# Moving one of three shifted additions from VectorE to GpSimd in an attention kernel

## The chip, the cores and the metric

The kernel runs on one core of one Trainium2 chip. The metric is the device time of one execution in microseconds (us). In the profile PE is TensorE (PEld its weight loads), DVE is VectorE, ACT is ScalarE, POOL is GpSimd, SP the engine that issues the DMAs. PSUM is the memory that PE writes its results to (the tiles psA, psD and psO here), SBUF the memory of all other tiles. The granted clock is the mean share of its full clock that PE was given in a run. A name such as L754 is a line of the kernel's source.

All full kernels were run two to four times, always next to runs of the kernel before on the same chip, and are compared with fast runs only; no run of them was slow (over 1.5% above the fastest of its kernel). A ratio of two kernels is the mean time of one kernel's runs over the mean of the other's of the same rounds, so it isn't quite the ratio of the medians that are quoted.

## The reference

```python
# B, H, S, Dh = 1, 32, 2048, 20; bfloat16
qn = q / (jnp.sqrt((q * q).sum(axis=-1, keepdims=True)) + eps)
kn = k / (jnp.sqrt((k * k).sum(axis=-1, keepdims=True)) + eps)
logits = jnp.einsum('bhqd,bhkd->bhqk', qn, kn) * t[None, :, None, None]
attn = _softmax(logits, axis=-1)
return jnp.einsum('bhqk,bhkd->bhqd', attn, v)
```

The heads are small (20 columns), so most of the work of ScalarE and VectorE is the exponential of 32 x 2048 x 2048 scores.

## The kernel before

Scores are made on PE in blocks of 128x512, 2048 blocks in all. Most go through ScalarE's exponential. The rest are taken by VectorE in tiles of four blocks, and it makes the exponential with integer arithmetic: it reads the scores from PSUM, scales them and writes int16 numbers that are, taken as fp16 bits, a piecewise linear 2^x. To smooth that curve, three copies of the tile are shifted by a quarter, a half and three quarters of an octave. PE sums all four, with the value rows scaled to undo the shift. This is that part (`# ...` marks cuts):

```python
PHASES = (256, 512, 768)
def add_dgroup(jg):
    # ... per tile two reads of PSUM, 1024 columns each:
    t1_prev[nchunk[0]] = add("DVE", f"t1.{j}.{k}", lambda e, tk, o=o, slot=slot: e.tensor_scalar(
        xt[sx][:, o:o + W1], psD[:, slot * W1:slot * W1 + W1], X_MUL, X_ADD, ALU.mult, ALU.add), ...)
    # ... three shifted copies of 2048 columns:
    sh = [dv(f"s{i}.", lambda e, tk, i=i: e.tensor_scalar(
        ss[i][se][:, 0:w], x, float(PHASES[i]), None, ALU.add), 0.533, ...) for i in range(len(PHASES))]
    # ... four groups of value matmuls, one for xt and one for each ss
```

GpSimd does little: it scales the value rows once for each head and phase.

```python
vsc[h] = [add("POOL", f"vs{h}", lambda e, tk, i=i: e.tensor_scalar(
    vph[bv][:, i, 0:nd, :], vaug[bv][:, R - nd:R, :], 2.0 ** (-PHASES[i] / 1024.0), 1.0, ALU.mult, ALU.mult), 0.5, ...)]
```

The kernel orders its instructions with a list scheduler of its own, which is given a duration for every task (the number after the function, in us) and emits a fixed order for each engine.

Of the kernel before, what the change touches and what calls it, by code (L numbers as in the profile page):

```python
# [26 lines left out]

class Task:
    __slots__ = ("eng", "fn", "dur", "deps", "pri", "name", "lat", "dma", "n", "users",
                 "start", "end", "seq", "inc", "cnt", "rows", "work", "modes")  # L30

    def __init__(self, eng, name, fn, dur, deps, pri, lat=0.0, dma=None):
        self.eng, self.name, self.fn, self.dur = eng, name, fn, dur
        self.deps = [d for d in deps if d is not None]
        self.pri, self.lat, self.dma = pri, lat, dma
        self.inc, self.cnt = False, 0
        self.rows, self.work, self.modes = 128, 512.0, None


class Program:  # L40
# [23 lines left out]
    def schedule(self):  # L64


        heavy = set()
        choice = [t for t in self.tasks if t.modes]
        for _ in range(self.PASSES):
            for t in choice:  # L70
                tag, t.rows, t.dur, t.work = t.modes[t in heavy]
                t.name = tag + t.name[2:]
            self.list_schedule()
            pe = [t for t in self.order["PE"] if t.end > self.LIGHT]
            more, i, load = set(), 0, 0.0
            work = [t.work for t in pe]
            for j, t in enumerate(pe):
                while pe[i].end < t.end - self.TICK:
                    load -= work[i]
                    i += 1  # L80
                for free in (True, False):
                    m = j - 1
                    while i and load < self.LOAD and m >= i:
                        u = pe[m]
                        if u.modes and u not in heavy and u not in more and (u.modes[1][2] == u.dur) == free:
                            more.add(u)
                            work[m] += u.modes[1][3] - u.work
                            load += u.modes[1][3] - u.work
                        m -= 1
                load += work[j]  # L90
            if not more:
                break
            heavy |= more
        self.heavy = heavy
        return self.order

    def list_schedule(self):
        for t in self.tasks:
            t.users = []
        for i, t in enumerate(self.tasks):  # L100
            t.seq = i
            deps = []
            for d in t.deps:
                deps += d() if callable(d) else [d]
            t.deps = list(dict.fromkeys(deps))
            t.n = len(t.deps)
            for d in t.deps:
                d.users.append(t)
        free = {}
# [15 lines left out]
        for t in self.tasks:  # L125
# [3 lines left out]
            if t.n == 0:  # L129
                arrive(t, 0.0)  # L130
        order = {e: [] for e in free}
        done = 0
        last_pe = [""]
        while events:
            now = events[0][0]
            touched = set()
            while events and events[0][0] <= now:
                _, kind, _, t = heapq.heappop(events)
                touched.add(t.eng)
                if kind == 0:  # L140
                    heapq.heappush(ready[t.eng], (t.pri, t.seq, t))
                    if t.eng in soon:
                        soon[t.eng].pop(t.seq, None)
            for e in touched:
                if free[e] > now + 1e-9 or not ready[e]:
                    continue
                held = []
                if e in soon:
                    held = [r for r in ready[e] if r[2].name[:2] not in ("t1", "tr") and
                            not (e == "PE" and r[2].name[0] == "q" and r[2].name[2] == "A") and hold(e, now, r[2].dur)]  # L150
                    if len(held) == len(ready[e]):
                        continue
                    if held:
                        ready[e] = [r for r in ready[e] if r not in held]
                        heapq.heapify(ready[e])
                if e == "PE":
                    x = min(ready[e], key=lambda r: (r[0] + (0.0 if r[2].name[:2] == last_pe[0] else self.SWITCH), r[1]))
                    ready[e].remove(x)
                    heapq.heapify(ready[e])
                    t = x[2]  # L160
                else:
                    _, _, t = heapq.heappop(ready[e])
                for r in held:
                    heapq.heappush(ready[e], r)
                t.start = now
                t.end = now + t.dur
                if e == "PE":
                    kind = t.name[:2]
                    if kind != last_pe[0]:
                        t.end += 0.09  # L170
                        self.nsw += 1
                    if now < self.PE_REST:
                        t.end += t.dur
                    last_pe[0] = kind
                free[e] = t.end
                order[e].append(t)
                done += 1
                heapq.heappush(events, (t.end, 1, t.seq, t))
                for u in t.users:
                    lat = t.lat if t.dma else (  # L180
                        self.SEM_LAT[e] if u.eng != e else 0.12 if e == "DVE" else 0.0)
                    if u.eng == "PE" and u.name[:2] == "pv":
                        lat += self.PV_SLACK
                    rt[u.seq] = max(rt[u.seq], t.end + lat)
                    u.n -= 1
                    if u.n == 0:
                        arrive(u, rt[u.seq])
        assert done == len(self.tasks), "dependence cycle"
        self.order = order
        return order  # L190
# [57 lines left out]
def bass_standalone__qk_norm__prompt_kernel(  # L248
# [13 lines left out]
    W1 = 1024  # L262
    LIGHT3 = True
    NP = 40
    NB = 6
    NV = 6
    NN = 4
    NT = 3
    NX = 4
    NE = 3  # L270
    GD = 1
    NWARM2 = 5
    NWARM = 15
# [4 lines left out]
    FIRST = -7.0  # L278
    DLEAD = 0.8
    PE_MM = 0.23  # L280
    MORE = 10
    DVE_TILES = [4 + (h * MORE // 31 > (h - 1) * MORE // 31 if h else 0) for h in range(H)]
    NDMAX = 5

    with ExitStack() as es:
        sbuf = lambda name, shape, dt: es.enter_context(nc.sbuf_tensor(name, shape, dt))
# [27 lines left out]
        prog = Program()  # L314
        add = prog.add

        def dma(eng, name, dst, src, deps, pri, key, lat=2.2, dur=0.62):
            return add(eng, name, lambda e, tk: e.dma_start(dst, src), dur, deps, pri, lat=lat, dma=key)  # L318

        def memset(eng, ap, val, dur, pri):  # L320
# [65 lines left out]
        def add_loads(h):  # L386
            b, bv = h % NB, h % NV
            pri = h - LEAD - 0.5
            war = ([norm[h - NB]] if h >= NB else []) + ([lambda: [trn[h - 2]]] if h >= EARLY else [])
            x = qk_sb[b]  # L390
            lds[h] = [dma("SP", f"ldk{h}", x[:, R:2 * R, :], k[0, h].rearrange("(p r) d -> p r d", p=128),
                          war, pri - 0.01 if h else -50, f"k{b}")]
            if h == 0:
                lds[h].append(dma("ACT", "ldq0", x[:, 0:R, :], q[0, 0].rearrange("(p r) d -> p r d", p=128),
                                  [], -99, "q0a"))
            else:

                for nh in range(4):
                    src = bass.AP(q.tensor, q[0, h].offset + nh * D,
                                  [[16 * D, 32], [4 * D, 4], [512 * D, 4], [1, D]])  # L400
                    dst = x[32 * nh:32 * nh + 32, 0:R, :].rearrange("p (c g) d -> p c g d", g=4)
                    lds[h].append(dma("SP", f"ldq{h}", dst, src, war, pri, f"q{b}", lat=2.5))
            war = (pv_users[h - NV] if h >= NV else z_v[bv]) + ([lambda: [trn[h - 2]]] if h >= 2 else [])
            if h == 1:
                war = war + [lambda: [trn[0]]]
# [2 lines left out]
            nd = NDMAX if h == 0 else DVE_TILES[h]  # L408
            vsc[h] = [add("POOL", f"vs{h}", lambda e, tk, i=i: e.tensor_scalar(  # L409
                vph[bv][:, i, 0:nd, :], vaug[bv][:, R - nd:R, :], 2.0 ** (-PHASES[i] / 1024.0), 1.0, ALU.mult, ALU.mult),  # L410
                0.5, [ld_v[h]] + (pv_users[h - NV] if h >= NV else z_v[bv]), pri + 0.2) for i in range(len(PHASES))]

        def add_prep(hs):
            due = hs[0] - LEAD if hs[0] != 1 else FIRST
# [46 lines left out]
        def add_trn(h):  # L461
# [2 lines left out]
            war = [lambda: qk_users[h - NT] + rot[h - NT]] if h >= NT else []  # L464
            trn[h] = add("SP", f"trn{h}", lambda e, tk: e.dma_start_transpose(
                qkT[bt][:, :].rearrange("p (c n) -> p c n", n=128),
                qkn[b][:, :, :].rearrange("p r d -> p (r d)")), 1.3, [norm[h]] + war, due + 0.1, lat=2.2, dma=f"T{bt}")
            rot[h] = [dma("SP", f"qz{h}", qz[bt][32 * g:32 * g + 32, g, :], qkT[bt][32 * g:32 * g + 32, 0:512],
                          [trn[h], z_qz[bt]] + ([lambda: qk_users[0]] if h == NT else []), due + 0.15, f"Z{bt}") for g in range(NG)]

# [179 lines left out]
        def add_dgroup(jg):  # L650
# [32 lines left out]

            def dv(name, fn, dur, deps):
                return add("DVE", f"{name}{js[0]}", fn, 0.068 + dur * len(js), deps, due)
            sh = [dv(f"s{i}.", lambda e, tk, i=i: e.tensor_scalar(  # L686
                ss[i][se][:, 0:w], x, float(PHASES[i]), None, ALU.add), 0.533, t1s + old(f"s{i}", NE)) for i in range(len(PHASES))]
            dusers["x", jg] = list(sh)
            for nm, tile, dep, ph in [("x", xt[sx], t1s, None)] + [(f"s{i}", ss[i][se], [sh[i]], i) for i in range(len(PHASES))]:
                us = dusers.setdefault((nm, jg), [])  # L690
                for i, j in enumerate(js):
                    h, rg = D_tiles[j]
# [82 lines left out]
```

## Time and profile before

| kernel before | |
|---|---|
| time, median of the first three runs | 711.08 us (710.19 to 712.51) |
| ScalarE busy | 689.1 us, 97% of the profiled span of 712.0 us |
| VectorE busy | 684.5 us, 96% |
| PE / GpSimd busy | 633.1 us / 37.8 us |
| VectorE tiles | 138 of four blocks each |

The engine totals of the page (busy us, share of the span, number of instructions):

```profile
PE 633.1 (89%) x5715; PEld 168.6 (24%) x5780; DVE 684.5 (96%) x1041; ACT 689.1 (97%) x607; POOL 37.8 (5%) x116
```

The groups of instructions by shape (columns: line, engine, operation, out<-in, shapes and types, count, then busy us and mean ns of one, then idle time of the engine before them and what ended it):

```profile
L632 ACT ACTIVATE p_ring<-psA 128x1536 bf16<-128x1536 f32 x299 | 450.9, 1508 | 14.5 <-PE psA L546 13.5
L678 DVE TENSOR_SCALAR xt<-psD 128x1024 int16<-128x1024 f32 x276 | 335.5, 1216 | 7.6 <-PE psD L546 7.4
L632 ACT ACTIVATE p_ring<-psA 128x1024 bf16<-128x1024 f32 x299 | 324.6, 1086 | 2.0 <-PE psA L546 1.7
L686 DVE TENSOR_SCALAR ss<-xt 128x2048 int16<-128x2048 int16 x414 | 270.5, 682 | 0.1
...
L409 POOL TENSOR_SCALAR vph<-vaug 128x128 f16<-128x128 bf16 x63 | 22.5, 357 | 402.6 <-DMA vaug<-in_v_dram 399.3
...
L409 POOL TENSOR_SCALAR vph<-vaug 128x160 f16<-128x160 bf16 x33 | 12.2, 368 | 212.9 <-DMA vaug<-in_v_dram 211.2
```

ScalarE and VectorE are both full. To win time, work has to leave both: if VectorE gets lighter, tiles can move to it from ScalarE. In the last two lines GpSimd scales value rows, 128 elements in 357 ns and 160 in 368 ns.

Who waited for whom (total us, times, longest us):

```profile
ACT p_ring L632 <- PE psA L546: 15.2, 27, 1.7
DVE xt L678 <- PE psD L546: 7.4, 10, 2.0
...
DVE sq L426 <- DMA qk_sb<-in_q_dram: 5.5, 5, 2.2
```

The waits of the two full engines are small. Last, two stretches of the timeline (start us, duration us, engine and instruction). They show where GpSimd and VectorE meet:

```profile
303.87 0.69 DVE L686 TENSOR_SCALAR ss<-xt 128x2048 int16<-128x2048 int16 x1
303.91 1.54 POOL L409 TENSOR_SCALAR vph<-vaug 128x128 f16<-128x128 bf16 x3 [39.32 <-DMA vaug<-in_v_dram]
...
348.90 1.22 DVE L678 TENSOR_SCALAR xt<-psD 128x1024 int16<-128x1024 f32 x1
349.44 1.05 POOL L409 TENSOR_SCALAR vph<-vaug 128x128 f16<-128x128 bf16 x3 [39.55 <-DMA vaug<-in_v_dram]
350.03 0.81 DVE L428 TENSOR_REDUCE rs_sum<-sq 128x32 f32<-128x640 bf16 x1
```

Three scalings of GpSimd took 1.54 us where a shift of VectorE had started just ahead of them, and 1.05 us under a PSUM read and a reduction. This fits what the Trainium skill, "SBUF — State Buffer", section "Who interferes with whom", says of the port of SBUF that both engines share: a VectorE operation in a two-port mode and a GpSimd operation exclude each other, while one with at most one input from SBUF, outside of these modes, leaves the port to GpSimd. That a shift is of the first kind and a PSUM read of the second is at this point only suggested by the two stretches; e1 tests it.

### The profile page before, as it was taken

The page shows a single profiled execution, that of the slowest core. Times are in us where ns is not written, and L with a number is a line of the kernel's source. Part 1 is how long each engine was busy: PE and PEld are TensorE (multiplying, and loading weights), DVE is VectorE, ACT ScalarE, POOL GpSimd, SP SyncE. Part 2 cuts the span into 40 slices and gives each one's busy share as a digit, 9 for nine tenths or more (in the row PEclk, how much of TensorE's full clock was granted, in tenths as well). Part 3 has the DMA queues.
Part 4 walks back from the last instruction along what each step waited for, and adds up shares of the span by engine and source line. Part 5 has one row for each costly group of instructions (what it writes and reads, how often), then busy time and mean ns, then how long its engine had stood idle before and what let it go on. Part 6 is the DMA issues. An engine that isn't in the chain of part 4 may idle for free.

```text
span 712.0 us, 14025 instructions
## 1 busy us (share of the span) xinstructions
PE 633.1 (89%) x5715; PEld 168.6 (24%) x5780; DVE 684.5 (96%) x1041; ACT 689.1 (97%) x607; POOL 37.8 (5%) x116
## 2 busy tenths in 40 slices
PE   7888988898899988888989999898999899999897
PEld 2222222222222222222222222222222222222221
DVE  8999899998999999999999989999999899999996
ACT  8999999999899999999999999999999989999997
POOL 3010000101001010010100101000010000100000
PEclk9999999999999999999999999999999999999999
DMA  5332413334143241322413234241332513322100
GB/s 64 71 49 42 74 17 90 33 71 57 23 81 30 68 55 37 70 22 68 60 31 74 29 75 48 50 67 27 78 36 53 69 25 74 35 68 47 39 17 10
DMA packets 196720, 36.20 MB, mean 51 GB/s; under 512 B 172592, under 2 KB 196656, under 8 KB 196656
## 3 DMA queue, kind: packets, MB, share of 16 engines
q1 hardware_dynamic: 196512, 35.22, 30.1%
q8 instruction: 45, 0.74, 0.4%
q14 instruction: 19, 0.16, 0.1%
q10 hardware_dynamic: 144, 0.08, 0.0%
HBM read 7.87 MB, written 2.62 MB: 15 GB/s over the span
## 4 chain that ended last, share of the span: by engine, by line
DVE 41%; SPq 34%; ACT 11%; DMA 6%; issue 5%; PE 3%; ACTq 0%; DVEq 0%
SPq L318 34%; DVE xt L678 19%; DVE ss L686 12%; ACT p_ring L632 11%; DMA qk_sb<-in_q_dram 4%; DVE qkn L454 3%; DVE rs_sum L428 2%; DMA qkT<-qkn 1%; DVE sq L426 1%; DVE oT L577 1%; PE psA L546 1%; DVE o_stage L587 1%; PE psO L565 1%; PE psD L546 1%; DVE rs_b L438 1%
## 5 line engine op out<-in xcount | busy, mean ns | idle before, releaser
L632 ACT ACTIVATE p_ring<-psA 128x1024 bf16<-128x1024 f32 x599 | 682.3, 1296 | 16.5 <-PE psA L546 15.2
L678 DVE TENSOR_SCALAR xt<-psD 128x1024 int16<-128x1024 f32 x276 | 335.5, 1216 | 7.6 <-PE psD L546 7.4
L546 PE MATMUL psA<-qz,kR 64*128 64x512 bf16 (+2 forms) x1100 | 252.3, 385 | 23.0 <-ACT p_ring L632 17.4
L686 DVE TENSOR_SCALAR ss<-xt 128x2048 int16<-128x2048 int16 x414 | 270.5, 682 | 0.1
L565 PE MATMUL psO<-ss,vph 128*32 128x512 f16 x1656 | 152.7, 386 | 6.5 <-DVE ss L686 6.3
L565 PE MATMUL psO<-p_ring,vaug 128*32 128x512 bf16 x1496 | 133.8, 385 | 1.1 <-ACT p_ring L632 1.1
L546 PE MATMUL psD<-qz,kR 64*128 64x512 bf16 (+1 forms) x384 | 112.6, 386 | 24.0 <-DVE xt L678 16.0
L546 PE MATMUL psA<-qz,qkT 64*128 64x512 bf16 (+2 forms) x366 | 119.8, 384 | 9.7 <-ACT p_ring L632 7.1
L546 PEld LDWEIGHTS psA<-qz,kR 64*128 64x128 bf16 (+2 forms) x1122 | 59.3, 93 | 168.1 <-ACT p_ring L632 147.4
L409 POOL TENSOR_SCALAR vph<-vaug 128x128 f16<-128x128 bf16 (+1 forms) x96 | 34.6, 361 | 615.6 <-DMA vaug<-in_v_dram 610.5
L565 PEld LDWEIGHTS psO<-ss,vph 128*32 128x32 f16 x1656 | 37.7, 94 | 92.2 <-issue 52.2
L546 PE MATMUL psD<-qz,qkT 64*128 64x512 bf16 (+1 forms) x133 | 50.9, 386 | 8.5 <-DVE xt L678 4.7
L565 PE MATMUL psO<-xt,vaug 128*32 128x512 f16 x552 | 53.1, 390 | 0.1
L565 PEld LDWEIGHTS psO<-p_ring,vaug 128*32 128x32 bf16 x1496 | 35.7, 94 | 61.9 <-issue 51.4
L546 PEld LDWEIGHTS psD<-qz,kR 64*128 64x128 bf16 (+1 forms) x414 | 27.9, 95 | 86.2 <-DVE xt L678 78.0
L546 PEld LDWEIGHTS psA<-qz,qkT 64*128 64x128 bf16 (+2 forms) x374 | 29.8, 93 | 62.2 <-ACT p_ring L632 56.0
L577 DVE STREAM_TRANSPOSE oT<-psO 128x512 f32<-128x512 f32 x32 | 22.6, 707 | 4.3 <-PE psO L565 4.3
L426 DVE TENSOR_TENSOR sq<-qk_sb 128x640 bf16<-128x640 bf16 x32 | 15.5, 486 | 11.4 <-DMA qk_sb<-in_q_dram 5.5
L428 DVE TENSOR_REDUCE rs_sum<-sq 128x32 f32<-128x640 bf16 x32 | 25.9, 809 | 0.1
L454 DVE TENSOR_TENSOR qkn<-qk_sb,rs_r 128x640 bf16<-128x640 bf16 x31 | 25.1, 814 | 0.0
L565 PEld LDWEIGHTS psO<-xt,vaug 128*32 128x32 bf16 x552 | 13.5, 93 | 33.8 <-issue 24.2
L546 PEld LDWEIGHTS psD<-qz,qkT 128*128 128x128 bf16 (+1 forms) x138 | 12.9, 95 | 28.8 <-DVE xt L678 21.2
(40 smaller groups left out, 78.7 us busy)
## 6 DMA issues: line engine op xcount, KB each, us to landing
kR<-qkT SPq DMA_DIRECT2D x62, 96.0 KB, 2.1
qz<-qkT SPq DMA_DIRECT2D x124, 32.0 KB, 1.9
kR<-qkT SPq DMA_DIRECT2D x62, 64.0 KB, 2.0
qk_sb<-in_k_dram SPq DMA_DIRECT2D x32, 80.0 KB, 2.6
vaug<-in_v_dram SPq DMA_DIRECT2D x32, 80.0 KB, 3.3
qk_sb<-in_q_dram SPq DMA_DIRECT2D x124, 20.0 KB, 2.5
out_dram<-o_stage SPq DMA_DIRECT2D x31, 80.0 KB, 2.4
kR<-qkT SPq DMA_DIRECT2D x62, 32.0 KB, 1.9
```

Source lines behind the costliest of these rows:

```text
L318: return add(eng, name, lambda e, tk: e.dma_start(dst, src), dur, deps, pri, lat=lat, dma=key)
L409: vsc[h] = [add("POOL", f"vs{h}", lambda e, tk, i=i: e.tensor_scalar(vph[bv][:, i, 0:nd, :], vaug[bv][:, R - nd:R, :], 2.0 ** (-PHASES[i] ...
L426: s1 = dv("sq", lambda e, tk, x=x: e.tensor_tensor(sq[:, :, :], x[:, :, :], x[:, :, :], ALU.mult), 0.41, lds[h] + last_sum + (q0[2:] if h ...
L428: sums.append(dv("sum", lambda e, tk, i=i: e.tensor_reduce(rs["sum"][:, 2 * R * i:2 * R * (i + 1)], sq[:, :, :], AXIS_X, ALU.add), 0.73, [ ...
L438: c = dv("rs", lambda e, tk: e.scalar_tensor_tensor(rs["b"][:, 0:w], rs["a"][:, 0:w], -0.5, rs["sum"][:, 0:w], ALU.mult, ALU.mult), 0.07 + ...
L454: norm[h] = dv("norm", lambda e, tk, x=x, b=b, i=i: e.tensor_tensor(qkn[b][:, :, 0:D], x[:, :, :], bc(rs["r"][:, 2 * R * i:2 * R * (i + 1) ...
L546: return eng.matmul(dst, lhsT, mov, tile_position=(p0, 0))
L565: last = eng.matmul(psO[32 * g:32 * g + 32, :], w, rhs_of(g), start=start, stop=False, skip_group_check=True, tile_position=(0, 32 * g))
L577: trO[h] = add("DVE", f"tr{h}", lambda e, tk: e.transpose(oT[:, :, :].rearrange("p r d -> p (r d)"), psO[:, :]), 0.63, [lambda: pv_users[h ...
L632: act[w] = add("ACT", f"exp{w}", lambda e, tk: e.activation(p_ring[:, p0 * 512:p0 * 512 + n], psA[:, slot * WAVES[0] * 512:slot * WAVES[0] ...
L678: t1_prev[nchunk[0]] = add("DVE", f"t1.{j}.{k}", lambda e, tk, o=o, slot=slot: e.tensor_scalar(xt[sx][:, o:o + W1], psD[:, slot * W1:slot ...
L686: sh = [dv(f"s{i}.", lambda e, tk, i=i: e.tensor_scalar(ss[i][se][:, 0:w], x, float(PHASES[i]), None, ALU.add), 0.533, t1s + old(f"s{i}", ...
```

## The change

The intent is to take the third shift off VectorE. GpSimd makes it in two halves of 1024 columns for 134 of the tiles, and the scheduler starts each half so that, by the durations that it believes, it runs under a PSUM read, transpose or reduction of VectorE. The relieved VectorE gets 13 more tiles. Loads of queries and keys wait for the transpose four heads back instead of two, and there are more buffers. The diff, cut to its core:

```diff
-    NB = 6
+    NB = 8
-    NE = 3
+    NE = 4
-    MORE = 10
+    MORE = 23
-    NDMAX = 5
+    NDMAX = 6
+    NSH = 2
+    KD = 10
+    PCH, PDUR, PWIN = 1024, 1.02, 0.98
 # loads:
-            war = (...) + ([lambda: [trn[h - 2]]] if h >= EARLY else [])
+            war = (...) + ([lambda: [trn[max(0, h - 4)]]] if h >= EARLY else [])
 # ... scheduler: a GpSimd task with a window (t.win) is started only where it fits
 # ... under a running PSUM read, transpose or reduction of VectorE, and waits for the
 # ... VectorE instruction in front of it; later VectorE tasks keep clear of the window
+                fit = [r for r in ready["POOL"] if r[2].win and s + r[2].win <= span[1]]
 # ... the shifts:
+            for i in range(len(PHASES)):
+                if i < NSH or jg < 2 or jg % KD == KD - 1:
+                    sh.append([dv(...)])          # on VectorE as before
+                    continue
+                for c in range(0, w, PCH):
+                    u = add("POOL", f"s{i}.{js[0]}.{c}", lambda e, tk, i=i, dst=dst, c=c: e.tensor_scalar(
+                        dst[:, c:c + PCH], xt[sx][:, c:c + PCH], float(PHASES[i]), None, ALU.add), PDUR, war, due)
+                    u.win = PWIN
```

`PDUR` is the duration that the scheduler believes of one half, 1.02 us, and `PWIN` the time for which it keeps VectorE's shifts away from it. Cut from the diff are smaller parts of the change: other durations and delays that the scheduler believes of loads, transposes and scalings, and a window for the scalings too.

More of the change, by code (lines that the diff above doesn't have):

```diff
@@ L29 @@
     __slots__ = ("eng", "fn", "dur", "deps", "pri", "name", "lat", "dma", "n", "users",
-                 "start", "end", "seq", "inc", "cnt", "rows", "work", "modes")
+                 "start", "end", "seq", "inc", "cnt", "rows", "work", "modes", "win", "trig")
     def __init__(self, eng, name, fn, dur, deps, pri, lat=0.0, dma=None):
@@ L37, in __init__ @@
         self.rows, self.work, self.modes = 128, 512.0, None
+        self.win, self.trig = 0.0, None
 class Program:
@@ L94, in schedule @@
         self.heavy = heavy
+        for t in self.tasks:
+            if t.trig is not None:
+                t.deps.append(t.trig)
         return self.order
@@ L99, in list_schedule @@
             t.users = []
+            t.trig = None
         for i, t in enumerate(self.tasks):
@@ L131, in list_schedule, with leave, pool_fill @@
         order = {e: [] for e in free}
+        span = [0.0, 0.0]
+        def leave(t, now):
+            for u in t.users:
+                lat = t.lat if t.dma else (
+                    self.SEM_LAT[t.eng] if u.eng != t.eng else 0.12 if t.eng == "DVE" else 0.0)
+                if u.eng == "PE" and u.name[:2] == "pv":
+                    lat += self.PV_SLACK
+                rt[u.seq] = max(rt[u.seq], t.end + lat)
+                u.n -= 1
+                if u.n == 0:
+                    arrive(u, max(now, rt[u.seq]))
+        def pool_fill(now):
+            n = 0
+            while True:
+                s = max(now, free["POOL"], span[0])
+                fit = [r for r in ready["POOL"] if r[2].win and s + r[2].win <= span[1]]
+                if not fit:
+                    return n
+                x = min(fit)
+                ready["POOL"].remove(x)
+                heapq.heapify(ready["POOL"])
+                t = x[2]
+                d = order["DVE"]
+                i = len(d) - 2
+                if i > 0 and d[i].start - d[i - 1].end < 0.02 and d[i].name[0] == "s" and d[i + 1].start - d[i].end < 0.02:
+                    i -= 1
+                t.trig = d[i] if i >= 0 else None
+                t.start, t.end = s, s + t.dur
+                free["POOL"] = t.end
+                lock[0] = s + t.win
+                order["POOL"].append(t)
+                heapq.heappush(events, (t.end, 1, t.seq, t))
+                leave(t, now)
+                n += 1
+        lock = [0.0]
         done = 0
         last_pe = [""]
-        while events:
+        while events or ready["POOL"]:
+            if not events:
+                now = max(free.values())
+                span[:] = [now, now + 9.0]
+                done += pool_fill(now)
             now = events[0][0]
@@ L144, in list_schedule @@
             for e in touched:
-                if free[e] > now + 1e-9 or not ready[e]:
+                if e == "POOL":
+                    done += pool_fill(now)
+                if free[e] > now + 1e-9 or not ready[e] or e == "POOL" and all(r[2].win for r in ready[e]):
                     continue
@@ L160, in list_schedule @@
                     t = x[2]
+                elif e == "POOL":
+                    x = min(r for r in ready[e] if not r[2].win)
+                    ready[e].remove(x)
+                    heapq.heapify(ready[e])
+                    t = x[2]
                 else:
@@ L165, in list_schedule @@
                 t.start = now
-                t.end = now + t.dur
+                if e == "DVE":
+                    if t.name[:2] in ("t1", "tr", "su"):
+                        span[:] = [now, now + t.dur]
+                    else:
+                        t.start = max(now, lock[0])
+                t.end = t.start + t.dur
                 if e == "PE":
@@ L178, in list_schedule @@
                 heapq.heappush(events, (t.end, 1, t.seq, t))
-                for u in t.users:
-                    lat = t.lat if t.dma else (
-                        self.SEM_LAT[e] if u.eng != e else 0.12 if e == "DVE" else 0.0)
-                    if u.eng == "PE" and u.name[:2] == "pv":
-                        lat += self.PV_SLACK
-                    rt[u.seq] = max(rt[u.seq], t.end + lat)
-                    u.n -= 1
-                    if u.n == 0:
-                        arrive(u, rt[u.seq])
+                leave(t, now)
+                if e == "DVE" and span[0] == t.start:
+                    done += pool_fill(now)
         assert done == len(self.tasks), "dependence cycle"
@@ L315, in bass_standalone__qk_norm__prompt_kernel, with dma @@
         add = prog.add
-        def dma(eng, name, dst, src, deps, pri, key, lat=2.2, dur=0.62):
+        def dma(eng, name, dst, src, deps, pri, key, lat=2.2, dur=0.65):
             return add(eng, name, lambda e, tk: e.dma_start(dst, src), dur, deps, pri, lat=lat, dma=key)
@@ L388, in add_loads @@
             pri = h - LEAD - 0.5
-            war = ([norm[h - NB]] if h >= NB else []) + ([lambda: [trn[h - 2]]] if h >= EARLY else [])
+            war = ([norm[h - NB]] if h >= NB else []) + ([lambda: [trn[max(0, h - 4)]]] if h >= EARLY else [])
             x = qk_sb[b]
             lds[h] = [dma("SP", f"ldk{h}", x[:, R:2 * R, :], k[0, h].rearrange("(p r) d -> p r d", p=128),
-                          war, pri - 0.01 if h else -50, f"k{b}")]
+                          war, pri - 0.01 if h else -50, f"k{b}", lat=4.5 if h else 2.2)]
             if h == 0:
@@ L401, in add_loads @@
                     dst = x[32 * nh:32 * nh + 32, 0:R, :].rearrange("p (c g) d -> p c g d", g=4)
-                    lds[h].append(dma("SP", f"ldq{h}", dst, src, war, pri, f"q{b}", lat=2.5))
+                    lds[h].append(dma("SP", f"ldq{h}", dst, src, war, pri, f"q{b}", lat=4.5))
             war = (pv_users[h - NV] if h >= NV else z_v[bv]) + ([lambda: [trn[h - 2]]] if h >= 2 else [])
@@ L410, in add_loads @@
                 vph[bv][:, i, 0:nd, :], vaug[bv][:, R - nd:R, :], 2.0 ** (-PHASES[i] / 1024.0), 1.0, ALU.mult, ALU.mult),
-                0.5, [ld_v[h]] + (pv_users[h - NV] if h >= NV else z_v[bv]), pri + 0.2) for i in range(len(PHASES))]
+                0.4, [ld_v[h]] + (pv_users[h - NV] if h >= NV else z_v[bv]), pri + 0.2) for i in range(len(PHASES))]
+            for u in vsc[h] if h else []:
+                u.win = 0.36
         def add_prep(hs):
@@ L466, in add_trn @@
                 qkT[bt][:, :].rearrange("p (c n) -> p c n", n=128),
-                qkn[b][:, :, :].rearrange("p r d -> p (r d)")), 1.3, [norm[h]] + war, due + 0.1, lat=2.2, dma=f"T{bt}")
+                qkn[b][:, :, :].rearrange("p r d -> p (r d)")), 1.3, [norm[h]] + war, due + 0.1, lat=3.0, dma=f"T{bt}")
             rot[h] = [dma("SP", f"qz{h}", qz[bt][32 * g:32 * g + 32, g, :], qkT[bt][32 * g:32 * g + 32, 0:512],
@@ L685, in dv @@
                 return add("DVE", f"{name}{js[0]}", fn, 0.068 + dur * len(js), deps, due)
-            sh = [dv(f"s{i}.", lambda e, tk, i=i: e.tensor_scalar(
-                ss[i][se][:, 0:w], x, float(PHASES[i]), None, ALU.add), 0.533, t1s + old(f"s{i}", NE)) for i in range(len(PHASES))]
-            dusers["x", jg] = list(sh)
-            for nm, tile, dep, ph in [("x", xt[sx], t1s, None)] + [(f"s{i}", ss[i][se], [sh[i]], i) for i in range(len(PHASES))]:
+            sh = []
+            for i in range(len(PHASES)):
+                dst, war = ss[i][se], t1s + old(f"s{i}", NE)
+                if i < NSH or jg < 2 or jg % KD == KD - 1:
+                    sh.append([dv(f"s{i}.", lambda e, tk, i=i, dst=dst: e.tensor_scalar(
+                        dst[:, 0:w], x, float(PHASES[i]), None, ALU.add), 0.533, war)])
+                    continue
+                sh.append([])
+                for c in range(0, w, PCH):
+                    u = add("POOL", f"s{i}.{js[0]}.{c}", lambda e, tk, i=i, dst=dst, c=c: e.tensor_scalar(
+                        dst[:, c:c + PCH], xt[sx][:, c:c + PCH], float(PHASES[i]), None, ALU.add), PDUR, war, due)
+                    u.win = PWIN
+                    sh[-1].append(u)
+            dusers["x", jg] = [u for us in sh for u in us]
+            for nm, tile, dep, ph in [("x", xt[sx], t1s, None)] + [(f"s{i}", ss[i][se], sh[i], i) for i in range(len(PHASES))]:
                 us = dusers.setdefault((nm, jg), [])
```

## The prediction

> **What bounds the kernel now.** Two engines at once. Engine totals: ACT 689.1 us busy (97% of 712.0) and DVE 684.5 (96%), PE 633.1, POOL 37.8. In the groups by shape ACT spends 682.3 us on 1496 exponential blocks of 128x512: 0.456 us a block. DVE turns the other 552 blocks (138 tiles) into fp16 bits: per tile two PSUM reads (pitch in the timeline 1.13 us) and three shifted additions of 128x2048 (pitch 0.60 us). ACT waits 15.2 us for PE's psA scores, DVE 7.4 us for psD and 11.4 us at the squares, mostly for loads. The chain of waits spends 34% of the span in the DMA queue: loads wait for a transpose two heads back.
>
> **What moves.** The changed kernel's instruction order shows 302 PSUM reads (276 before), 319 shifts on DVE (414) and 268 half shifts of 128x1024 on POOL. So 13 tiles, 52 blocks, leave ACT.
> - ACT: 52 x 0.456 = -23.7 us, to about 665 busy.
> - DVE: +26 x 1.13 - 95 x 0.60 = -27.6 us, to about 657.
> - PE: each moved tile needs four value-matmul groups instead of one: 13 x 3 x about 0.23 us (estimate from 386 ns matmuls that overlap) = +9 us, in the slack of an engine at 89%.
> - POOL: three 128x128 scalings take 1.05 us undisturbed and three 128x160 take 1.13, so an estimate by slope is 1.0 to 1.1 us per half; 268 of them are about 280 us, 320 with the scalings.
>
> **The risk is the shared port.** The Trainium skill, "SBUF — State Buffer", section "Who interferes with whom", says that GpSimd and a two-port DVE operation exclude each other for a whole instruction, while a PSUM read leaves the port free. The trace agrees: three scalings took 1.05 us at 349.4 us, under a PSUM read and a reduction, but 1.54 us at 303.9 us, where a shift of 0.69 us ran first. A half of 1.0 to 1.1 us just fits under a PSUM read of 1.13 us; each overrun delays the next DVE shift. I allow 0.03 to 0.05 us on average, 8 to 13 us of DVE time. Second cost: psD is single-buffered. 44 gaps between PSUM reads now hold one shift alone, 7 nothing; before, four gaps with one shift measured 1.73 to 1.99 us from read to read, so up to 0.25 us lost in each, 0.6 in each empty one: about 8 us more DVE waiting.
>
> **Critical path.** DVE: 657 + 27 idle + 8 + 10 = about 702 at worst, 690 if the earlier loads remove most of the 11 us at the squares. ACT: 665 + 23 idle = 688.
>
> **Prediction: 692 us (ratio 0.973), range 682 to 706.** Faster by over 2% (below 696.9): 0.62; within 2%: 0.32; slower: 0.06.
>
> **What would show it right or wrong.** ACT busy 663 to 668, its wait for psA 15 to 30 us. DVE busy 655 to 672; shifts keep a mean near 0.68 us (right) or show 0.75 and more (port blocking: wrong). DVE wait for psD 10 to 20 us. Squares wait for loads under 5 us. Value matmuls seldom wait on POOL. PE busy about 640, clock near 0.99.
>
> **What would make it wrong.** Halves of 1.2 us or more would block a shift every time and give back 25 us: no gain. POOL falling behind its schedule, so that xt buffers (four) are not free and PSUM reads wait.

## The result

The changed kernel took 915.5 us (median of 4 runs, 912.9 to 917.2; before 711.8 us), a ratio of 1.286 with a 95% interval of 1.281 to 1.291. It is correct, and 29% slower.

The engine totals of the changed kernel:

```profile
PE 695.7 (76%) x5880; PEld 174.6 (19%) x5936; DVE 779.9 (85%) x972; ACT 683.9 (75%) x586; POOL 831.3 (91%) x384
```

GpSimd went from 37.8 to 831.3 us and is now the fullest engine, at 91%. The part of the page with the chain that ended last says which engine the time follows:

```profile
POOL 72%; DVE 13%; PE 10%; issue 4%; POOLq 0%; DMA 0%
```

The groups by shape (same columns as before):

```profile
L754 POOL TENSOR_SCALAR ss<-xt 128x1024 int16<-128x1024 int16 x268 | 788.5, 2963 | 50.0 <-DVE ss L749 17.9 <-DVE oT L636 8.8 <-DVE rs_b L497 6.7
L691 ACT ACTIVATE p_ring<-psA 128x1536 bf16<-128x1536 f32 x288 | 420.0, 1458 | 181.2 <-PE psA L605 170.5 <-PE psO L624 8.3 <-PE psD L605 1.6
...
L749 DVE TENSOR_SCALAR ss<-xt 128x2048 int16<-128x2048 int16 x319 | 284.2, 908 | 1.2
```

A half takes 2963 ns in the mean, where the prediction had 1000 to 1100. VectorE's shifts went from 682 to 908 ns. The view of that one line of the source gives the durations of the halves (ns, minimum/median/maximum):

```profile
L754 POOL TENSOR_SCALAR ss<-xt x268: 2762/2824/3700, 24.5 to 905.6; 128x1024 int16<-128x1024 int16 x134
```

This line tells much before any experiment. The minimum and the median are nearly the same, 2762 and 2824 ns. If another engine stretched the halves, some of the 268 would probably have escaped it; e1 tests this.

Who waited for whom after the change:

```profile
PEld psO L624 <- POOL ss L754: 212.0, 117, 5.1
ACT p_ring L691 <- PE psA L605: 202.3, 183, 4.6
PE psO L624 <- POOL ss L754: 168.1, 107, 4.6
...
DVE xt L737 <- PE psD L605: 109.3, 85, 5.0
```

PE waits for GpSimd's halves (its weight loads 212.0 us, its matmuls 168.1 us; the two may overlap and are not added). The scheduler gave PE a fixed order, so while it stands there it makes no scores, and ScalarE waits 202.3 us for them and VectorE 109.3 us. ScalarE's busy time fell to 683.9 us only, though 52 blocks left it: with 912.7 - 683.9 = 228.8 us of idle time, fewer of its instructions overlap (their durations sum to 718.6 us for 677.2 us of busy time, and to 775.5 for 682.3 before). The lower granted clock of PE (0.90 against 0.995) came with its waits; no run here separates the two.

### The profile page after: what moved, and what is told of

The parts are those of the page before. It is cut to its first block, busy times and chain, and to the rows that moved or that the text cites. A ratio compares the mean times of both kernels' runs of the same rounds, so it can differ in the third digit from the quotient of the medians.

```text
span 912.7 us, 14481 instructions
## 1 busy us (share of the span) xinstructions
PE 695.7 (76%) x5880; PEld 174.6 (19%) x5936; DVE 779.9 (85%) x972; ACT 683.9 (75%) x586; POOL 831.3 (91%) x384
## 4 chain that ended last, share of the span: by engine, by line
POOL 72%; DVE 13%; PE 10%; issue 4%; POOLq 0%; DMA 0%
POOL ss L754 70%; DVE xt L737 5%; PE psO L624 5%; DVE ss L749 4%; PE psA L605 3%; POOL vph L466 2%; PE psD L605 2%; DVE oT L636 1%; DVE rs_sum L487 1%; DVE qkn L513 1%; DVE sq L485 0%; POOLq L342 0%; DVE rs_a L495 0%; DVE rs_b L497 0%; DMA qk_sb<-in_k_dram 0%
## 5 line engine op out<-in xcount | busy, mean ns | idle before, releaser
L691 ACT ACTIVATE p_ring<-psA 128x1024 bf16<-128x1024 f32 x578 | 677.2, 1243 | 216.9 <-PE psA L605 202.3
L754 POOL TENSOR_SCALAR ss<-xt 128x1024 int16<-128x1024 int16 x268 | 788.5, 2963 | 50.0 <-DVE ss L749 17.9
L737 DVE TENSOR_SCALAR xt<-psD 128x1024 int16<-128x1024 f32 x302 | 366.8, 1215 | 110.5 <-PE psD L605 109.3
L624 PE MATMUL psO<-ss,vph 128*32 128x512 f16 x1812 | 188.1, 426 | 169.1 <-POOL ss L754 168.1
L749 DVE TENSOR_SCALAR ss<-xt 128x2048 int16<-128x2048 int16 x319 | 284.2, 908 | 1.2
L605 PE MATMUL psD<-qz,kR 64*128 64x512 bf16 (+1 forms) x438 | 134.1, 413 | 16.6 <-DVE xt L737 11.1
L605 PE MATMUL psA<-qz,qkT 64*128 64x512 bf16 (+2 forms) x350 | 129.6, 416 | 6.1 <-ACT p_ring L691 2.7
L624 PEld LDWEIGHTS psO<-ss,vph 128*32 128x32 f16 x1812 | 44.8, 97 | 281.2 <-POOL ss L754 212.0
L605 PEld LDWEIGHTS psA<-qz,kR 32*128 32x128 bf16 (+2 forms) x1083 | 57.4, 95 | 157.0 <-ACT p_ring L691 83.5
L624 PE MATMUL psO<-xt,vaug 128*32 128x512 f16 x604 | 65.4, 423 | 0.2
L466 POOL TENSOR_SCALAR vph<-vaug 128x160 f16<-128x160 bf16 (+2 forms) x96 | 39.7, 413 | 26.5 <-DMA vaug<-in_v_dram 10.9
L605 PEld LDWEIGHTS psD<-qz,qkT 64*128 64x128 bf16 (+1 forms) x151 | 14.4, 96 | 30.4 <-DVE xt L737 17.2
```

The lines of the kernel that those rows point to most:

```text
L605: return eng.matmul(dst, lhsT, mov, tile_position=(p0, 0))
L624: last = eng.matmul(psO[32 * g:32 * g + 32, :], w, rhs_of(g), start=start, stop=False, skip_group_check=True, tile_position=(0, 32 * g))
L691: act[w] = add("ACT", f"exp{w}", lambda e, tk: e.activation(p_ring[:, p0 * 512:p0 * 512 + n], psA[:, slot * WAVES[0] * 512:slot * WAVES[0] ...
L749: sh.append([dv(f"s{i}.", lambda e, tk, i=i, dst=dst: e.tensor_scalar(dst[:, 0:w], x, float(PHASES[i]), None, ALU.add), 0.533, war)])
L754: u = add("POOL", f"s{i}.{js[0]}.{c}", lambda e, tk, i=i, dst=dst, c=c: e.tensor_scalar(dst[:, c:c + PCH], xt[sx][:, c:c + PCH], float(PHA ...
```

## The experiments

The question is which step failed: the duration of a half, the shared port, or the loads and buffers. Three theories of the duration were on the table at first: the type int16, the stretching by VectorE, or the size alone.

### e1: the instruction by itself

Not an edit of the kernel, but a small program: GpSimd makes each form three times with all else quiet, then six halves beside VectorE's shifts, six beside PSUM reads, and single halves with a shift that starts a set time after them.

```python
ts = lambda src, n, s1, s2, o0, o1=None: ...   # e.tensor_scalar on n columns
forms.append(("i16add1024", I16, 1024, ts(xi, 1024, 256.0, None, ALU.add)))
forms.append(("f16add1024", FP16, 1024, ts(xf, 1024, 1.0, None, ALU.add)))
forms.append(("i16multmult1024", I16, 1024, ts(xi, 1024, 1.0, 1.0, ALU.mult, ALU.mult)))
forms.append(("tti32add512", I32, 512, lambda e, d: e.tensor_tensor(d, xw, cw, ALU.add)))
# ... 17 forms
```

> A measurement of the disputed instruction by itself; it computes nothing of the reference (output zero, wrong on purpose). POOL alone makes each form three times, then six int16 halves alone, beside 30 shifts of VectorE, beside 16 PSUM reads, then six fp16 halves beside 30 shifts, then single halves with a shift that arrives after a PSUM read of 128 to 2048 columns. Theory A (the int16 type makes the half slow): the int16 128x1024 addition alone takes about 2.7 us and the fp16 one about 1.0 us. Theory B (the half is about 1.0 us and VectorE's use of the shared port stretches it): the int16 half alone takes about 1.0 us and about 2.8 us beside the shifts. Theory C (size alone, whatever the type): the fp16 half takes about 2.7 us too. For the port: if a half holds it for its whole duration, a shift that arrives 0.2 us after the half starts is delayed by about 2.5 us; if it holds it only while it reads, by about 0.8 us.

The groups by shape of that program (pSHIFT are halves beside shifts, pREAD beside PSUM reads, q_ the forms alone):

```profile
L81 POOL TENSOR_SCALAR pSHIFT<-xi 128x1024 int16<-128x1024 int16 x6 | 20.5, 3436 | 0.6 <-DVE trg L118 0.6
L81 POOL TENSOR_SCALAR pREAD<-xi 128x1024 int16<-128x1024 int16 x6 | 16.4, 2768 | 7.3 <-DVE trg L118 7.3
L29 POOL TENSOR_SCALAR q_i16addadd<-xi 128x1024 int16<-128x1024 int16 x3 | 10.8, 3631 | 0.0
L30 POOL TENSOR_SCALAR q_i16add<-xi 128x1024 int16<-128x1024 int16 x3 | 8.2, 2769 | 20.9 <-DVE x L105 20.9
L30 POOL TENSOR_SCALAR q_f16add<-xf 128x1024 f16<-128x1024 f16 x3 | 8.2, 2769 | 0.0
...
L46 POOL TENSOR_TENSOR q_tti32add<-xw,cw 128x512 int32<-128x512 int32 x3 | 3.7, 1259 | 0.0
L29 POOL TENSOR_SCALAR q_i16multmult<-xi 128x1024 int16<-128x1024 int16 x3 | 3.1, 1044 | 0.0
...
L29 POOL TENSOR_SCALAR q_bf2f16multmult<-xb 128x1024 f16<-128x1024 bf16 x3 | 3.1, 1044 | 0.0
...
L30 POOL TENSOR_SCALAR q_i16add<-xi 128x128 int16<-128x128 int16 x3 | 1.5, 527 | 0.0
...
L29 POOL TENSOR_SCALAR q_bf2f16multmult<-xb 128x128 f16<-128x128 bf16 x3 | 0.8, 297 | 0.0
```

The half takes 2.77 us alone, and the same beside PSUM reads. Beside an unbroken row of shifts it takes 3.44 us, so VectorE adds about a quarter there. The type makes no difference: int16 and fp16 both take 2769 ns. So the first two theories fall. The third falls too, as the same 1024 int16 elements take 1044 ns when they are multiplied twice, and 3631 ns when two additions are asked for. What decides is the operation. A lone addition costs (2769 - 527) / 896 = 2.50 ns an element, two multiplications (1044 - 297) / 896 = 0.83 ns. GpSimd's old work, the scaling of value rows, is of the second kind, and the prediction had taken its slope.

The timeline of one slow half, and of the three shifts that VectorE made from 0.03 us after its start:

```profile
199.47 3.07 POOL L81 TENSOR_SCALAR pALONE<-xi 128x1024 int16<-128x1024 int16 x1 [7.27 <-DVE trg L118]
199.50 1.56 DVE L114 TENSOR_SCALAR vSHIFT<-yi 128x2048 int16<-128x2048 int16 x1
200.98 0.68 DVE L114 TENSOR_SCALAR vSHIFT<-yi 128x2048 int16<-128x2048 int16 x1
201.58 1.51 DVE L114 TENSOR_SCALAR vSHIFT<-yi 128x2048 int16<-128x2048 int16 x1
```

The first shift ended about 0.88 us later than one of 0.68 us would have, the second ran undisturbed in the middle of the half, and the third lost another 0.83 us. So a slow half keeps VectorE's shifts waiting in two stretches of 0.8 to 0.9 us, and not for all of its 3.07 us.

### e2: the loads and buffers alone

```diff
-    MORE = 23
+    MORE = 10
-    NSH = 2
+    NSH = 3
```

> The changed kernel with all three shifts on VectorE and the old number of VectorE tiles (138): the earlier loads and more buffers alone. If the loss comes from POOL's halves alone: 700 to 712 us, VectorE's waits at the squares under 5 us. If the loads or the buffers are part of the loss: over 725 us.

It took 705.3 us (ratio 0.987, interval 0.985 to 0.989), correct. The wait of VectorE's squares for loads, 5.5 us before, no longer appears among its waits, as predicted. The run keeps all else of the change too, the scheduler's new durations among it. Together these parts are a gain of 1.3%, not part of the loss; what each of them brings was not tested.

### e3: the halves as fp16

```diff
-   dst[:, c:c + PCH], xt[sx][:, c:c + PCH], float(PHASES[i]), None, ALU.add
+   dst[:, c:c + PCH].bitcast(FP16), xt[sx][:, c:c + PCH].bitcast(FP16), float(PHASES[i]), None, ALU.add
```

> The changed kernel with the same bytes and the same halves on POOL, but read and written as fp16 (wrong result on purpose). Theory A (int16 is what makes a half slow): halves of 1.0 to 1.1 us, POOL no longer behind, 685 to 705 us as the prediction had it. Theories B and C: halves of 2.8 us and 900 us as before.

It took 914.5 us, with halves of 2955 ns. Its output is wrong, which doesn't matter for the time. The type is not the cause, in the full kernel as in e1.

### e4: the halves as 32-bit integer additions

```diff
-   e.tensor_scalar(dst[:, c:c + PCH], xt[sx][:, c:c + PCH], float(PHASES[i]), None, ALU.add)
+   e.tensor_tensor(dst[:, c:c + PCH].bitcast(I32), xt[sx][:, c:c + PCH].bitcast(I32), cw[:, 0:PCH].bitcast(I32), ALU.add)
```

The tile `cw` holds the phase in every int16. The Trainium skill, "GPSIMD Engine Reference", section "Engine selection", states that such an addition of one 32-bit integer type is exact. Two int16 numbers lie in one word, and no carry passes between them as all sums are positive int16.

> The changed kernel with each half as an integer addition of 512 32-bit words and a constant tile (two int16 in a word, no carry between them, so the result stays right). Estimate from half the elements with two inputs: 1.1 to 1.5 us a half. Theory A with type conversion as the cost: about 700 us, perhaps below before. If each 32-bit word is as slow as two int16: 2.7 us and about 900 us.

It took 695.5 us (ratio 0.973, interval 0.971 to 0.976), and the result is correct, which agrees with that statement. The two groups of interest (same columns):

```profile
L756 POOL TENSOR_TENSOR ss<-xt,cw 128x512 int32<-128x512 int32 x268 | 390.2, 1457 | 207.6 <-DVE ss L751 82.2 <-DVE qkn L515 27.2 <-DVE oT L638 18.8
...
L751 DVE TENSOR_SCALAR ss<-xt 128x2048 int16<-128x2048 int16 x319 | 216.6, 696 | 1.2
```

Alone such a half takes 1259 ns (e1), here 1457 ns in the mean, inside the 1.1 to 1.5 us that were expected. Only the halves and the making of `cw` differ from the changed kernel, so nearly all of the loss lies in the halves.

### e5: which operations are fast

The same program as in e1 with other pairs of operations.

> A second measurement of POOL's forms by themselves (wrong output on purpose). The first one gave 2.77 us for 1024 elements with an addition in every type, and 1.04 us with two multiplications. Theory D1 (the addition is slow, in whatever place): multiply-then-add, add-then-multiply, subtract and a lone add all take 2.7 us or more; a lone multiply 1.0 us. Theory D2 (only the form with an empty second operation is slow): a lone multiply takes 2.7 us too, multiply-then-add about 1.0 us. Theory D3 (multiply-then-multiply alone is fast): everything else 2.7 us or more. It also places a shift of VectorE 0.03, 0.4 and 1.0 us after the start of a multiplying half and of a 32-bit integer half: if both hold the port in one stretch of about 0.9 us, the first shift is delayed by about 0.9, 0.5 and 0 us.

The groups by shape of the second program, the names giving the two operations:

```profile
L29 POOL TENSOR_SCALAR q_multsub<-xi 128x1024 int16<-128x1024 int16 x3 | 10.8, 3638 | 0.0
...
L30 POOL TENSOR_SCALAR q_multnone<-xi 128x1024 int16<-128x1024 int16 x3 | 8.2, 2771 | 0.0
...
L30 POOL TENSOR_SCALAR q_addnone<-xi 128x1024 int16<-128x1024 int16 x3 | 8.2, 2769 | 0.0
...
L29 POOL TENSOR_SCALAR q_multadd<-xi 128x1024 int16<-128x1024 int16 x3 | 3.1, 1044 | 0.0
L29 POOL TENSOR_SCALAR q_addmult<-xi 128x1024 int16<-128x1024 int16 x3 | 3.1, 1043 | 0.0
```

None of the three theories is right as it was put. A lone multiplication is as slow as a lone addition (2771 and 2769 ns), and a lone subtraction or maximum took the same, so the addition is not what is slow. But an empty second operation isn't the whole rule either: multiply-then-subtract takes 3638 ns. Of the forms tried, multiply-multiply, multiply-add and add-multiply were fast, at 1043 to 1055 ns (the last for a multiply-add of fp16), and each of the others of one input and 1024 elements took 2.77 us or more, apart from a plain copy (1037 ns in e1). Why is not visible in a trace.

A fast half and a shift that starts 0.03 us after it:

```profile
186.25 1.04 POOL L80 TENSOR_SCALAR pALONE<-xi 128x1024 int16<-128x1024 int16 x1 [7.27 <-DVE trg L121]
186.28 1.56 DVE L117 TENSOR_SCALAR vSHIFT<-yi 128x2048 int16<-128x2048 int16 x1
```

The shift ended about 0.88 us late, after which the port was free. In the same run five shifts took 3.08 us when the first started 0.96 us after the start of a fast half, 3.57 us when it started 0.42 us after that, and 3.97 us at 0.03 us. The fast half thus keeps shifts waiting in one stretch that ends about 0.9 us after its start, and the window of 0.98 us in the changed kernel covers it.

### e6: multiply by one, then add

```diff
-   xt[sx][:, c:c + PCH], float(PHASES[i]), None, ALU.add), PDUR, war, due)
+   xt[sx][:, c:c + PCH], 1.0, float(PHASES[i]), ALU.mult, ALU.add), PDUR, war, due)
```

> The changed kernel with each half as (x times 1.0) plus the phase, the same numbers out (result right). D1 and D3: halves of 2.7 to 3.6 us, 900 to 1000 us. D2: halves of 1.04 us and 685 to 700 us.

It took 683.8 us (ratio 0.955, interval 0.953 to 0.958), and the result is correct. It beats the kernel before by 4.5%, and lies just below the 685 to 700 us that D2 had. Its engine totals, the two groups that changed, and the waits that matter:

```profile
PE 639.1 (94%) x5936; PEld 171.0 (25%) x5936; DVE 665.7 (98%) x972; ACT 662.4 (97%) x586; POOL 370.7 (54%) x384
```

```profile
L754 POOL TENSOR_SCALAR ss<-xt 128x1024 int16<-128x1024 int16 x268 | 328.4, 1226 | 244.3 <-DVE ss L749 96.0 <-DVE qkn L513 31.3 <-DVE oT L636 20.6
...
L749 DVE TENSOR_SCALAR ss<-xt 128x2048 int16<-128x2048 int16 x319 | 213.4, 687 | 1.2
```

```profile
ACT p_ring L691 <- PE psA L605: 6.9, 7, 5.1
...
DVE xt L737 <- PE psD L605: 5.2, 11, 0.8
...
PEld psO L624 <- POOL ss L754: 3.0, 3, 1.5
```

Halves take 1226 ns in the mean, more than the 1.04 us that was expected; the shortest is 1038 ns. In the timeline one that started at 299.60 us, under a shift that had begun at 299.43, took 1.42 us, so a longer one seems to include a wait for the port. VectorE's shifts are back at 687 ns, and PE hardly waits for GpSimd. Between 915.5 and 683.8 us lies no other edit than the multiplication by 1.0.

### e7: two multiplications

```diff
-   xt[sx][:, c:c + PCH], float(PHASES[i]), None, ALU.add), PDUR, war, due)
+   xt[sx][:, c:c + PCH], 1.0, 1.0, ALU.mult, ALU.mult), PDUR, war, due)
```

> The changed kernel with each half as x times 1.0 times 1.0 (wrong result on purpose), everything else the same. If the duration of a half is the only step of the prediction that failed: halves of about 1.04 us, 685 to 697 us. If the fine interleaving fails for other reasons too (port blocking, psD): above 705 us.

It took 683.4 us, with halves of 1225 ns and a result that is wrong. It agrees with e6.

### e8 and e9: half of the tiles, and a scheduler that knows

Both keep the slow halves, but only for every second tile. In e9 the scheduler is also told their true duration.

```diff
-    KD = 10
+    KD = 2
-    PCH, PDUR, PWIN = 1024, 1.02, 0.98
+    PCH, PDUR, PWIN = 1024, 2.80, 0.98      # e9 only
```

> The changed kernel with POOL's slow halves for every second tile only (about 150 halves), VectorE makes the rest. If POOL's own pace (268 times 2.9 us) is what sets 912 us: POOL leaves the chain, and the time falls to 740 to 780 us, where VectorE, with 59 more shifts and those that the halves block, is the limit. If blocked shifts were the main cost rather than POOL's pace: the fall is no more than in proportion, to about 820 us.

> Half of the tiles on POOL with the slow halves, as in the run of 805 us, but the kernel's own list scheduler is told 2.80 us for a half instead of 1.02, so it places the value matmuls that need them later. If the 805 us came from PE waiting in order for halves that the schedule believed done: PE's waits for POOL fall from 172 us to under 40, and the time to 720 to 760 us, limited by VectorE with blocked shifts. If the wait comes from POOL's capacity or from blocked shifts: still about 800 us.

e8 took 805.3 us, between its two forecasts (740 to 780 us if GpSimd's pace set the time, about 820 if blocked shifts were the main cost), although GpSimd was busy only 504.6 of 802.9 us. e9 took 761.9 us, just above what was expected. PE's waits for GpSimd in e8:

```profile
PEld psO L624 <- POOL ss L754: 97.6, 61, 5.3
...
PE psO L624 <- POOL ss L754: 74.6, 58, 5.0
```

and in e9:

```profile
PEld psO L624 <- POOL ss L754: 13.7, 5, 7.2
PE psO L624 <- POOL ss L754: 11.7, 2, 6.7
```

So GpSimd's capacity is not the only cost of a slow half. In e8 it had spare time, and PE still stood waiting, because the order of its instructions was made for halves of 1.02 us. With the true duration in the scheduler those waits went from 97.6 and 74.6 us to 13.7 and 11.7 us, and the time fell by 43 us. Not all of this need be PE's waits: in the new order VectorE's shifts took 747 ns in the mean instead of 793, an estimated 378 x 0.046 = 17 us of its time. Of the 78 us that e9 still takes longer than e6, VectorE can account for about 58: its 59 more shifts at a pitch of 0.60 us are an estimated 35 us, and 378 shifts that are 747 - 687 = 60 ns longer are 23 us; its busy time is 724.5 us against 665.7. The other 20 us were not traced to a cause. The expectation of e8 had costed pace and port, but not the order; with the order mended, the time lies in the range that e8 was expected in.

### e10: all slow halves, with the true duration in the scheduler

```diff
-    PCH, PDUR, PWIN = 1024, 1.02, 0.98
+    PCH, PDUR, PWIN = 1024, 2.80, 0.98
```

> The changed kernel with all 268 slow halves, its scheduler told 2.80 us. POOL's pace alone needs 268 times 2.77 plus about 40 us, 782 us: 790 to 850 us if POOL's pace sets the time; the difference to 912 us would be the price of the wrong duration in the schedule.

It took 1435 us, far outside the expectation, and correct. GpSimd was busy for only 811.4 us of it, and ScalarE waited 716.9 us for value matmuls in 32 waits, the longest 45.7 us. It seems that more work was asked of GpSimd than fits under VectorE's reads, so that the scheduler set the heads behind one another; that was not tested. So it doesn't tell what GpSimd's pace alone would have cost, and the split of the 912.7 us into pace and order stays open.

### e11: fast halves without the extra tiles

e6 with `MORE = 10`, so 138 tiles as before.

> The fast halves (multiply by one, add the phase), but with the old number of VectorE tiles, 138. ScalarE then has its old 1496 blocks: about 700 to 706 us, the same as with the earlier loads alone (705), as shifts taken off VectorE buy nothing until tiles move. If VectorE was the tighter of the two: under 695 us.

It took 709.3 us (ratio 0.995, interval 0.992 to 0.998), just above the 700 to 706 us expected and slightly slower than the loads alone (705.3 us); why is open. VectorE fell to 631.1 us busy (one of its waits, for a load, was 15.6 us long), ScalarE stayed at 685.9 us. So the relief of VectorE alone buys nothing; the 13 tiles that it makes room for are the gain, from 709.3 to 683.8 us.

## Why the prediction was wrong

It said 692 us, in a range of 682 to 706, and 915.5 us was measured. Point by point:

- **The step that failed** is the term "an estimate by slope is 1.0 to 1.1 us per half; 268 of them are about 280 us, 320 with the scalings". The slope came from scalings with two multiplications and was used for a lone addition. Measured, a half takes at least 2.76 us, 2.96 in the mean; 268 of them filled 788.5 us, and GpSimd was busy for 831.3 us instead of 320. e6 and e7 show that no other step was needed for the miss: with the fast operations and all else as in the change, the time is 683.8 and 683.4 us, inside the stated range.
- **The warning was named but mis-sized.** The prediction said that halves of 1.2 us or more would "give back 25 us: no gain". It counted only blocked shifts. Its limit was too low: halves of 1226 ns in the mean (e6) and of 1457 ns (e4) left shifts of 687 and 696 ns, and both kernels gained. Its cost was too small for halves of 2963 ns: they also made PE wait in order, and through it ScalarE and VectorE, a loss of some 200 us and not 25. e8 and e9 show that the order is a real part of it, since 43 us came from it at half the tiles. The second warning, "POOL falling behind its schedule", came true, but by another path than the one named: no PSUM read waited for GpSimd to free an xt buffer; they waited 109.3 us for PE.
- **"Value matmuls seldom wait on POOL": wrong in the changed kernel**, where 117 of their weight loads and 107 of the matmuls waited (212.0 and 168.1 us); right in e6, with 3 weight loads and 3.0 us.
- **ACT -23.7 us, to about 665 busy: right once the halves are fast.** e6 shows 662.4 us. In the changed kernel as run, the idle ScalarE showed 683.9.
- **DVE -27.6 us, to about 657, and 655 to 672 in the profile: right in e6**, 665.7 us, with shifts of 687 ns against the stated 0.68 us. In the changed kernel they took 908 ns, the sign that the prediction had set for port blocking.
- **The wait for psD of 10 to 20 us: too high.** It was 5.2 us in e6. Gaps with one shift or none cost less than the 8 us allowed. This, and a port allowance of about 10 us that was hardly needed (shifts 5 ns longer than before, an estimated 2 us in all), may account for e6 lying 8 us below the 692 that was predicted.
- **PE about 640 busy in its slack: right in e6**, 639.1 us.
- **Earlier loads remove the waits at the squares: right.** e2 shows no such wait on loads, and 705.3 us.
- **The shared port under a PSUM read: right.** e1 shows halves of 2768 ns beside PSUM reads, as alone. The port was not the cause of the loss, but part of it: shifts were 226 ns longer in the mean, an estimated 319 x 0.226 = 72 us of VectorE's time, in a kernel where VectorE was no longer the limit.

## What to carry to other kernels

A duration measured for one operation of an engine need not hold for another on the same engine, even with the same shape and type (1044 against 2769 ns here): before work is moved to GpSimd, measure the very instruction by itself, and try a form with the same numbers out, such as multiply by one and add. Where a static order is made from assumed durations, a wrong one can cost twice, once as work and once as in-order waiting on other engines. Look at the minimum and the median of a group's durations first: when they are close, as 2762 and 2824 ns here, the instruction is probably slow by itself, which a run of it alone then confirms (2769 ns in e1).

## What the Trainium skill lacked or had wrong

- "GPSIMD Engine Reference", section "Engine selection", says of elementwise work that one-input operations are "roughly line-rate". The runs show no one rate for them: a plain copy of 1024 elements took 1037 ns, and the cost was 0.83 ns an element for multiply-multiply, with multiply-add and add-multiply as fast at 1024 elements, but 2.50 ns an element for a lone addition, and 2.77 us for 1024 elements with any of the four lone operations tried. That is slower than a two-input fp16 addition of the same length (2123 ns in e5).
- No page has the fast pairs: 1043 to 1055 ns for 1024 elements with multiply-multiply, multiply-add and add-multiply, 3631 and 3638 ns with add-add and multiply-subtract.
- "SBUF — State Buffer", section "Who interferes with whom", says that the pair is held for the whole instruction. A lone addition of about 2.8 to 3.1 us blocked VectorE's shifts in two stretches of 0.83 to 0.9 us and let one run in between; a multiplying one of 1.04 us blocked them until about 0.9 us after its start.
- The same section's statement that a VectorE instruction with at most one SBUF input, outside the two-port modes, does not contend agrees with the runs for PSUM reads, which the section does not name: 2768 ns beside PSUM reads, 2769 alone.
